# A planned order of all work: one PSUM bank kept for the zero matmuls, less slack behind transfers, and a new order

## The chip, the cores and the metric

The kernel runs on one core of a Trainium2 chip. The metric is device time in microseconds (us) of one execution. A core has five engines with an instruction stream each: TensorE (PE, matrix multiplication into PSUM), VectorE (DVE), ScalarE (ACT), GpSimd (POOL) and SyncE (SP). In this kernel POOL issues all loads, SP issues the stores and the crossbar transposes, and all transfers share 16 DMA engines. PSUM has eight banks of 128 x 512 fp32.

## The reference

Two stages. First a linear attention with an exponential feature map, over 8 batches of 8 heads, 576 tokens, head width 64 and 128 features; then a feed-forward network (FFN) with squared ReLU on 4608 tokens of width 512, inner width 2048.

```python
def phi(x):
    proj = np.einsum('bhsd,df->bhsf', x, w_phi)
    proj = proj - np.max(np.abs(proj), axis=-1, keepdims=True)
    return np.concatenate([np.exp(proj), np.exp(-proj)], axis=-1)
q_p, k_p = (phi(q), phi(k))
kv = np.einsum('bhsf,bhsd->bhfd', k_p, v)
z = np.sum(k_p, axis=2)
num = np.einsum('bhsf,bhfd->bhsd', q_p, kv)
den = np.einsum('bhsf,bhf->bhs', q_p, z)[..., None] + 1e-06
attn = num / den
x = attn.transpose(0, 2, 1, 3).reshape(B * S, H * D)
h = np.maximum(x @ w_in, 0.0)
out = h * h @ w_out
```

All inputs and outputs are fp32; the kernel computes in bf16 and accumulates in fp32.

## The kernel before

The kernel doesn't issue its work in program order. It first describes every operation in a `Plan` (engine, cost, what it reads and writes, which PSUM banks it opens and closes, and a key). `Machine` then plays the plan through once, on the host, at build time: each engine takes the operation with the lowest key among those that are ready, with PSUM banks handed out to PE operations and transfers sharing the DMA engines. What comes out is one order for each engine, and the instructions are written in exactly that order. On the chip each engine goes through its list in order, and waits with semaphores for what an instruction needs. The times of `Machine` fix the order and nothing else, with two exceptions. Loads are held back by a gate, the ACT operation that ends last before the planned start of the load. And zero matmuls are put where PE is planned to idle.

The keys stand in a table `KEYS`, 1739 of them, one for each operation; `RELEASES` has the earliest planned starts of the loads of batches 2 to 7; `STATES` says for each copy or ReLU that either ACT or DVE can do which of the two does it. `SLACK` is added to the planned end of a transfer, by its kind: `first` for the first loads and the weights, `v0` for the first v, `ld` for the loads of batches 2 to 7, `kq` for the crossbar transposes of k and q, `x` for those of the attention's output.

The zero matmuls keep PE busy while it has nothing to do. Before the change the bank they write is any that is planned to be free when PE comes to idle; if none is, there are no zero matmuls in that gap:

```python
spare = next((b for b in range(self.BANKS) if self.free_at[b] <= e["free"] + 1e-9), None) if name == "PE" else None
```

They are written out ahead of each PE operation that is planned before 45 us (`WARM_UP`), as many as fit into the planned gap, at 0.11 us each in the first 6 us and 0.058 us after.

The steps of a batch, with the lines of the kernel before:

- Loads of q, k and v, with a cast to bf16, by POOL (L512, L520, L532); weights (L581, L587).
- Transposes of k and q to kT and qT. In batches 0 and 1 PE does them (L616) with a copy out of PSUM by DVE or ACT (L439, L441); in batches 2 to 7 the crossbar does them (L626).
- Projections of k and q (L670 and L816 in batch 0, L642 elsewhere) that use half of the array's rows, row maxima of their absolute values (DVE L677, L722, L823), exponentials (ACT L705, L728), and v scaled with the exponentials of the maxima (DVE L762, L766).
- KV: 18 matmuls for each pair of heads (L783, L788), 4 pairs to a batch, and a copy to SBUF (L439, L441).
- The features of q, transposed (PE L858, ACT L873), numerators and denominators (PE L888, twice 8 matmuls, with a DVE operation L900 between), the division (DVE L908, L912) and a transpose of the result to xT: on PE (L928, copies L937) in batch 0, by crossbar (L950) elsewhere.
- The FFN in 9 chunks of 512 tokens: first product L1049 in chunk 0 (128 tokens at a time) and L1038 elsewhere, ReLU on ACT (L1015) or DVE (L1017), square on DVE (L1024), second product L1103 (L1067 for the last 128 tokens), copy and store (L1121). Chunk c needs the attention of batch c; the ninth chunk takes the last 64 tokens of all batches.

The FFN of a batch runs among the attention of the following ones. The first FFN matmul, L1049, comes after the attention of batch 0, for which q, k and v must be loaded first.

Of the kernel before, what the change touches and what calls it, by code (L numbers as in the profile page):

```python
# [21 lines left out]
SLACK = {"first": 1.2, "v0": 2.5, "ld": 0.8, "x": 1.2, "kq": 1.0}  # L22
# [3 lines left out]
WARM_UP, COLD = 45.0, 6.0  # L26
# [87 lines left out]
class Machine:  # L114
# [7 lines left out]
    def __init__(self, plan, limits, ahead, patience, want):  # L122
        self.plan, self.limits = plan, limits
        self.ahead, self.patience, self.want = ahead, patience, want
        self.free_at = [0.0] * self.BANKS
        self.holding = None
        self.open = {}
        self.q = {"SP": [], "POOL": []}
        self.q_t, self.q_v = 0.0, 0
        self.hist = {"SP": [], "POOL": []}  # L130
# [64 lines left out]
    def run(self):  # L195
# [81 lines left out]
        while left:  # L277
# [19 lines left out]
            spare = next((b for b in range(self.BANKS) if self.free_at[b] <= e["free"] + 1e-9), None) if name == "PE" else None  # L297
            op = pick(name, e, t)
# [52 lines left out]
def kernel(  # L351
# [245 lines left out]
    def attention(b):  # L597
        s2 = b % 2
        pe_in = b in K['PE_IN']
        first = b == 0  # L600
# [23 lines left out]
        def transposed(x, xt, tag, ttag, key):  # L624
            def fn():
                pin(nc.sync.dma_start_transpose(out=xt, in_=x))  # L626
            add("SP", (2.8 if tag == "xk" else 3.4, 0), key, fn, r=of(tag, b, (0, 1, "s") if tag == "xq" else (0, 1, 2, 3, "s")),
                w=[(ttag, s2, t) for t in range(18)], dma=(3.6, HW_IN, "x", "kq"), what="X" + tag)

        if not pe_in:  # L630
            transposed(xk[s2], kTb, "xk", "kT", KA(b) - 10)
            transposed(xq[s2], qTb, "xq", "qT", KA(b) - 9)
# [345 lines left out]
        else:  # L978
            if pe_in:
# [235 lines left out]
    'PE_IN': [0, 1],  # L1215
    'PX': [1, 1, 1, 1, 1],
# [5 lines left out]
    'LIM': {'b0': 7, 'att': 3, 'kv': 7, 'op': 6},  # L1222
    'AHEAD': 356.131,
    'PATIENCE': 60.701,
# [4 lines left out]
    '1000000100001001111000110100100000000100010000001001000000010101000010000010001000010010000010000000'  # L1229
    '0100000101001010001110100010101001001000100010011001000101001001101010010100101101100010010100011100'  # L1230
    '0111010111100111100110100000111'
# [3 lines left out]
    17407, 102, 303, -19, 23448, 164, 25399, 7284, 103, -334, -342, 962, 612, -4448, -358, -466, 854, -5120, 1043,  # L1235
    1445, 2531, 2378, 1835, 1683, 1283, 2296, 2776, 6225, 1578, 6847, 9430, 23446, 3002, 6973, 2986, 4636, 7251,
    4704, 6911, 3336, 1003, 977, 1014, 1256, 2044, 19225, 3264, 1208, 2649, 9653, 3031, 2018, 7283, 1699, 1392,
    2415, 2482, 2569, 1938, 7416, 2230, 19677, 19665, 21149, 985, 631, 1829, 1167, 502, 1106, 30444, 1429, 24788,
    11688, 1068, 2741, 2271, 1691, 557, 1483, 638, 1830, 1651, 599, -401, 1899, 768, 1607, 1345, 1946, 17315, 1356,
    23984, 24358, 2102, 2748, 1812, 1047, 7206, 3044, 7208, 17205, 16309, 2884, 1937, 2580, 2117, 23465, 1319,  # L1240
    32941, 353, 6936, 22713, 1482, 1252, 12153, 9984, 23851, 1776, 1870, 28693, 2989, 3338, 9168, 2470, 2176, -1818,
    1746, -2214, 2184, 2431, 2073, 16742, 12309, 3675, 32055, 2751, 2607, 33525, 19924, 2061, 1353, 18117, 879, 666,
    2992, 2848, 2951, 3261, 32406, -843, 2706, 724, 5383, 2189, 3713, -1132, 3059, 22482, 2647, 33607, 2425, 2903,
    3153, 7467, 2946, 17043, 887, 30937, 1975, 19418, 5174, 20405, 3839, 537, 22061, 13862, 4153, 4372, 3313, 3702,
    2934, 2946, 2343, 3093, 22612, 3559, 8512, 2725, 3616, 26332, 29011, 3758, 20842, 6383, 2667, 4917, 3013, 11902,
    5345, 5238, 5921, 9912, 17625, 6541, 2315, 4379, 3435, 538, 4929, 3936, -2259, 3063, 3410, 4141, 23913, 13791,
    14506, 9834, 3978, 4002, 4288, 4215, 2945, 1909, 5362, 5104, 5553, 5287, 3268, 17046, 798, 3707, 2741, -1094,
    3553, 8533, 6784, 7264, 5884, 4403, 7199, 11290, 5958, 4782, 5787, 5872, 5644, 5916, 5299, 5137, 5079, 5080,
    20856, -473, 6391, 5749, 5537, 5046, 6063, 19035, 3357, 9582, 5994, 4922, 5968, 6119, 4977, 6670, 6244, 6483,
    6290, 6698, 19067, 4958, -996, 5517, 5252, 5391, 6788, 5266, 4299, 5039, 2805, 10740, 5284, 7476, 6917, 6887,  # L1250
    9690, 7248, 39413, 1751, 9675, 6437, 28262, 6319, 5577, 6334, 6287, 6302, 18429, 7382, 2955, 6913, 5198, 24236,
    28571, 6767, 6251, 7494, -758, 7560, 8050, 9450, 7621, 8371, 7966, 3353, 2499, 2619, 1952, 6194, 29465, 774,
    5220, 3223, 3756, 4311, 3208, 4062, 4051, 4788, 3955, 479, 4014, 3767, 3800, 3168, 4377, -1024, 4889, 5051,
    4450, 2778, 4515, 7272, 9663, 4340, 4251, 5804, 5006, 4304, 9662, 4907, 2794, 5997, 5050, 5175, 5451, 4923,
    28317, 7970, 4699, 4303, 1709, 9057, 5944, 5392, 4331, 14380, 2713, 4765, 4953, 12329, 4480, 5767, 4592, 6860,
    7810, 10905, 2818, 6137, 4180, 2215, 3286, 7321, 5283, 5241, 5956, 5275, 31537, 7305, 7279, 8169, 7954, 8774,
    7928, 7946, 7447, 7197, 8571, 8788, 8754, 9914, 9151, 8623, 10205, 28753, 9236, 8038, 8574, 22052, 8380, 8450,
    7529, 3291, -2, 11359, 9824, 9084, 13735, 9213, 10106, 8801, 8580, 8548, 9717, 12195, 21514, 9841, 10195, 9372,
    20619, 10629, 7364, 7402, 8587, 6358, 6839, 7541, 9500, 9718, 10799, 10955, 10544, 5683, 2374, 9755, 9159,
    27351, 9417, 9862, 9302, 20470, 32494, 10238, 6138, 7030, 7927, 10849, 9641, 9510, -1016, 20794, 10915, 8427,  # L1260
    -116, 13197, 9447, 9495, 2667, 692, 22484, 20389, 10746, 7094, 9290, 10721, 10810, 18159, 12068, 31380, 28083,
    22915, 1026, -887, 11060, 3635, 11045, 11396, 9857, 12004, 7583, 18462, 8756, 4983, 7513, 8752, 3219, 5133,
    6755, -1, 15253, 5347, 6465, 7754, 11386, 4931, 4785, 5572, 8512, 18443, 10833, 15727, 7521, 27495, 8162, 6150,
    7496, 8751, 8038, 7422, 7940, 3836, 10117, 6091, 22706, 7326, 7703, 13090, 9732, 23399, 8450, 13984, 975, 23532,
    8575, 9687, 9024, 7376, 8938, 10675, 9574, 7478, 8651, 8128, 8849, 5308, 31332, 21114, 8850, 29038, 9584, 6298,
    9555, 13221, 10146, 26486, 9580, 10029, 16988, 7506, 5719, 7874, 7841, 7758, 7389, 9044, 16298, 13239, 12245,
    23349, 9079, 12781, 7480, 11973, 8824, 8823, 6561, 6517, 9711, 10208, 3635, 14886, 9819, 5468, 9796, 10776,
    9740, 9730, 27385, 11031, 18006, 10703, 10132, 14, 10657, 9648, 22562, 10246, 19975, 11130, 25441, 23920, 14604,
    8983, 8228, 15704, 10056, 12998, 9196, -1267, 15126, 10713, -326, 20534, 11321, 11509, 12968, 13034, 11538,
    4820, 11603, 1244, 11706, 11438, 11864, 10659, 15019, 12774, 13092, 11103, 11910, 12865, 11965, 11827, 10973,  # L1270
    -497, 11622, 13807, 31538, 11957, 13552, 5263, 12566, 12058, 10811, 25517, 12045, 9673, -2199, 12689, 6817,
    12468, 25073, 13804, 12710, 12761, 14880, 24784, 5370, 9220, 9204, 17211, 13305, -10, 31398, 22456, 9554, 20134,
    14287, 12831, 14375, 12743, 12421, 8816, 16805, 13198, 13168, 9775, 28439, 11026, 24020, 13360, 3050, 15853,
    1925, -239, 4903, 4986, 16708, 13835, 12965, 12562, 11651, 12912, 24547, -1847, 13009, 10966, -2373, 11087,
    9756, 10945, 10200, 12118, 10502, 10956, 21707, 16803, 17099, 11772, 18442, 13381, 11449, 31507, 22778, 12610,
    11775, 11507, 4434, 11804, 11515, 11801, -528, 11413, 13866, 16900, 5711, 15578, 9473, 13709, 19170, 12569,
    10487, 13433, 22777, 22857, 1833, 12762, 24856, 12485, 11283, 14167, 10087, 13341, 8113, 15210, 20080, 16461,
    14025, 15631, 11608, 14097, 7884, 30686, 20661, 25313, -255, -2159, 24682, 11371, 10070, 11200, 16134, 3932,
    16133, 5138, 7416, 7851, 16122, 8358, 8893, 11490, 11992, 12992, 8029, 10687, 6778, 8395, 11617, 11959, 12312,
    760, 4160, 11884, 14072, 15705, 3017, 16120, 11618, 13974, 4928, 13054, 13063, -961, 9709, 13238, 14877, 14414,  # L1280
    14408, 13167, 12813, 14444, 12170, 14604, 5327, 24549, 24508, 27999, 22376, 15936, 15990, 10069, 14146, 14114,
# [97 lines left out]
```

## Time and profile before

| | |
|---|---|
| time, median of 3 | 361.92 us (361.62 to 363.95) |
| span in the profile | 360.4 us |
| PE busy | 346.7 us, 3442 matmuls |
| DVE busy | 292.5 us, 503 instructions |
| ACT busy | 231.9 us, 434 instructions |
| POOL busy | 112.5 us, 167 instructions |
| zero matmuls (L1195) | 118 |
| DMA | 39.62 MB, mean 110 GB/s |

Busy time on PE is not time at PE's peak: a matmul of 512 columns is shown as 379 ns long while the next one starts 216 ns after it. So the distance between starts tells more than the busy share. `PEclk` gives the clock that PE was granted, in tenths of the full one, in 40 slices of 9 us. A row of the table by stretch has first the stretch and its length, then busy us and instructions of PE, PE's weight loads, DVE, ACT and POOL, then PE's clock, the DMA share (16 engines; it counts queues that overlap, so it goes above 1) and GB/s.

### The profile page before, as it was taken

The page shows a single profiled execution, that of the slowest core. Times are in us where ns is not written, and L with a number is a line of the kernel's source. Part 1 is how long each engine was busy: PE and PEld are TensorE (multiplying, and loading weights), DVE is VectorE, ACT ScalarE, POOL GpSimd, SP SyncE. Part 2 cuts the span into 40 slices and gives each one's busy share as a digit, 9 for nine tenths or more (in the row PEclk, how much of TensorE's full clock was granted, in tenths as well). Part 3 has the DMA queues.
Part 4 walks back from the last instruction along what each step waited for, and adds up shares of the span by engine and source line. Part 5 has one row for each costly group of instructions (what it writes and reads, how often), then busy time and mean ns, then how long its engine had stood idle before and what let it go on. Part 6 is the DMA issues. An engine that isn't in the chain of part 4 may idle for free.

```text
span 360.4 us, 8594 instructions
## 1 busy us (share of the span) xinstructions
PE 346.7 (96%) x3442; PEld 198.0 (55%) x3442; DVE 292.5 (81%) x503; ACT 231.9 (64%) x434; POOL 112.5 (31%) x167
## 2 busy tenths in 40 slices
PE   8579999999999999999999999999999999999995
PEld 8368886554554555446544555565455554444444
DVE  4998999899999977899789888999788965686131
ACT  2986899598888783959677847957785340310310
POOL 8626727366636951363415212010000000000000
PEclk9959999999999999999999999999999999999999
DMA  8999999998999999898847774447230031100213
GB/s 96 194 201 136 188 182 117 169 150 107 164 154 126 153 129 188 167 139 121 98 102 96 128 98 104 93 69 122 81 96 2 17 95 45 36 0 2 112 33 89
DMA packets 102632, 39.62 MB, mean 110 GB/s; under 512 B 77249, under 2 KB 98113, under 8 KB 102593
## 3 DMA queue, kind: packets, MB, share of 16 engines
q0 software_dynamic: 51744, 18.36, 47.3%
q1 hardware_dynamic: 50608, 20.55, 25.4%
q8 instruction: 27, 0.44, 0.5%
q10 hardware_dynamic: 240, 0.16, 0.2%
q14 instruction: 13, 0.10, 0.1%
HBM read 36.77 MB, written 9.44 MB: 128 GB/s over the span
## 4 chain that ended last, share of the span: by engine, by line
PE 75%; DVE 11%; ACT 9%; issue 2%; DMA 1%; POOL 0%; DVEq 0%; POOLq 0%; ACTq 0%
PE psum L1103 29%; PE psum L1038 24%; PE psum L888 5%; PE psum L783 4%; DVE mq L823 4%; PE psum L642 3%; PE psum L858 3%; PE psum L1049 2%; ACT kp L728 2%; DVE mk L722 2%; DVE va L766 2%; ACT kn L728 2%; DMA xq<-in_q_dram 1%; DVE h L1024 1%; PE psum L1067 1%
## 5 line engine op out<-in xcount | busy, mean ns | idle before, releaser
L1103 PE MATMUL psum<-wout,h 128*128 128x512 bf16 x560 | 131.5, 379 | 0.0
L1038 PE MATMUL psum<-xT,win 128*128 128x512 bf16 x448 | 105.0, 379 | 0.6 <-ACT hr L1015 0.4
L1015 ACT ACTIVATE hr<-psum 128x512 bf16<-128x512 f32 x91 | 53.6, 598 | 49.7 <-PE psum L1038 26.1
L1103 PEld LDWEIGHTS <-h 128*128 128x128 bf16 x560 | 50.7, 98 | 56.9 <-issue 2.7
L1038 PEld LDWEIGHTS <-win 128*128 128x128 bf16 x512 | 47.5, 98 | 53.6 <-issue 1.6
L1024 DVE TENSOR_TENSOR h<-hr 128x512 bf16<-128x512 bf16 x144 | 56.9, 416 | 16.2 <-ACT hr L1015 15.3
L873 ACT ACTIVATE qp<-psum 128x1024 bf16<-128x1024 f32 (+1 forms) x40 | 37.3, 938 | 20.0 <-PE psum L858 17.4
L532 POOL DMA_DIRECT2D xq<-in_q_dram x52 | 37.6, 726 | 39.1 <-ACT hr L1015 10.3
L823 DVE TENSOR_REDUCE mq<-psum 128x8 f32<-128x1024 f32 (+1 forms) x40 | 43.7, 1110 | 4.6 <-PE psum L642 3.7
L1017 DVE TENSOR_SCALAR hr<-psum 128x512 bf16<-128x512 f32 x53 | 36.1, 683 | 9.8 <-PE psum L1038 8.3
L722 DVE TENSOR_REDUCE mk<-psum 128x8 f32<-128x1024 f32 (+1 forms) x35 | 38.1, 1108 | 2.4 <-PE psum L642 1.7
L728 ACT ACTIVATE kp<-psum 128x1024 bf16<-128x1024 f32 (+1 forms) x35 | 32.8, 937 | 10.2 <-DVE mk L722 10.2
L766 DVE TENSOR_TENSOR va<-xv,va 128x1024 bf16<-128x1024 bf16 (+1 forms) x36 | 38.6, 1101 | 0.6 <-ACT va L747 0.4
L873 ACT ACTIVATE qn<-psum 128x1024 bf16<-128x1024 f32 (+1 forms) x40 | 37.4, 940 | 2.0 <-PE psum L888 2.0
L900 DVE TENSOR_TENSOR psum<-psum,en 128x520 f32<-128x520 f32 (+1 forms) x40 | 27.9, 700 | 7.4 <-PE psum L888 6.4
L728 ACT ACTIVATE kn<-psum 128x1024 bf16<-128x1024 f32 (+1 forms) x35 | 32.9, 948 | 0.1
L912 DVE TENSOR_TENSOR xo<-psum,rden 128x512 bf16<-128x512 f32 (+1 forms) x40 | 27.3, 687 | 0.9
L512 POOL DMA_DIRECT2D xv<-in_v_dram x26 | 18.9, 727 | 28.9 <-ACT qp L873 10.5
L512 POOL DMA_DIRECT2D xk<-in_k_dram x28 | 20.2, 721 | 21.9 <-ACT va L747 7.4
L783 PE MATMUL psum<-va,kp 128*128 128x65 bf16 x256 | 21.1, 199 | 0.1
L783 PE MATMUL psum<-va,kn 128*128 128x65 bf16 x256 | 20.9, 198 | 0.1
L441 ACT ACTIVATE ot<-psum 128x512 f32<-128x512 f32 x24 | 14.4, 603 | 10.0 <-PE psum L1103 6.8
(68 smaller groups left out, 407.4 us busy)
## 6 DMA issues: line engine op xcount, KB each, us to landing
out_dram<-ot SPq DMA_DIRECT2D x32, 256.0 KB, 2.6
xk<-in_k_dram POOLq DMA_DIRECT2D x26, 128.0 KB, 4.4
xv<-in_v_dram POOLq DMA_DIRECT2D x24, 128.0 KB, 4.4
xq<-in_q_dram POOLq DMA_DIRECT2D x48, 64.0 KB, 3.4
win<-in_moe_w_in_dram POOLq DMA_DIRECT2D x4, 512.0 KB, 11.0
wout<-in_moe_w_out_dram POOLq DMA_DIRECT2D x4, 512.0 KB, 7.7
xq<-in_q_dram POOLq DMA_DIRECT2D x4, 256.0 KB, 7.5
xv<-in_v_dram POOLq DMA_DIRECT2D x2, 512.0 KB, 8.5
```

The costliest lines, as they stand in the source:

```text
L512: pin(nc.gpsimd.dma_start(out=x[:, a * 512 : z * 512].rearrange("p (h x) -> p h x", x=4 * D), in_=src[b][2 * a : 2 * z, 0:512, :].rearrang ...
L532: pin(nc.gpsimd.dma_start(out=x[:, jj * 1024 + a * 256 : jj * 1024 + z * 256].rearrange("p (h x) -> p h x", x=128), in_=q[b][2 * a : 2 * z ...
L722: pin(nc.vector.tensor_reduce(out=mk_view(g), in_=ps2(pj)[:, :, : n * Fd].rearrange("p e (i f) -> p e i f", f=Fd), axis=AX.X, op=ALU.max, ...
L728: pin(nc.scalar.activation(out=dst[slot][:, :, :n, :].rearrange("p e i f -> p e (i f)"), in_=ps2(pj)[:, :, : n * Fd], func=ACT.Exp, scale= ...
L766: pin(nc.vector.tensor_tensor(out=o[:, :, :D], in0=xv[s2][:, 512 * g0 : 512 * g1].rearrange("p (m d) -> p m d", d=D), in1=o[:, :, D].to_br ...
L783: pin(nc.tensor.matmul(out=o[:, sg, hi, :], lhsT=(kp, kn)[sg][kgroup[pr]][:, j % 2, 2 * hi + j // 2, :], rhs=va[s2][sg_of(sg, pr)][:, 8 * ...
L823: pin(nc.vector.tensor_reduce(out=mqb[:, c, :, :n], in_=ps2(pj)[:, :, : n * Fd].rearrange("p e (i f) -> p e i f", f=Fd), axis=AX.X, op=ALU ...
L873: pin(nc.scalar.activation(out=o, in_=i_, func=ACT.Exp, scale=sgn))
L1015: pin(nc.scalar.activation(out=hr[sl], in_=ps1(g), func=ACT.Relu))
L1024: pin(nc.vector.tensor_tensor(out=dst, in0=i_, in1=i_, op=ALU.mult))
L1038: pin(nc.tensor.matmul(out=o, lhsT=win[mc // 4][:, kc, mc % 4 * P : (mc % 4 + 1) * P], rhs=x, start=(kc == 0), stop=(kc == KC - 1)))
L1103: pin(nc.tensor.matmul(out=ps1(g), lhsT=h2[c % 2][mc // 4][:, mc % 4, tt * P : (tt + 1) * P], rhs=wout[mc // 4][:, mc % 4, :], start=(mc = ...
```

## The change

Three edits of the planner, and the order that comes of them.

One bank, the eighth, is not handed out before 27 us of the plan (`RESERVED`), and zero matmuls planned before that time write it. So there is always a bank for them in the opening, at the price of one bank fewer for the work. 27 us is about where the FFN begins. The aim is that PE's clock stays up in the opening.

The slack behind transfers is smaller in all five kinds. The aim is that work is planned nearer to the time at which its data is there.

The switch `PE_IN` for batches whose q and k PE transposes is split in one for k (`PE_IN`) and one for q (`PE_Q`). Both name batches 0 and 1, so nothing is computed in another way.

With these a new set of keys, releases and states is given, so every engine's order differs: the order of loads in the opening, the place of each attention step in the FFN, and for some copies and ReLUs the engine (ReLU on DVE 57 times for 53, the output copy 9 times for 11). In the program that results PE has 3543 matmuls for 3442; all 101 more are zero matmuls. The limits on open banks by kind (`LIM`) and two settings of how PE groups its half-array work (`AHEAD`, `PATIENCE`) differ too.

```diff
-SLACK = {"first": 1.2, "v0": 2.5, "ld": 0.8, "x": 1.2, "kq": 1.0}
+SLACK = {"first": 0.6, "v0": 1.0, "ld": 0.6, "x": 1.0, "kq": 0.8}
...
-WARM_UP, COLD = 45.0, 6.0
+WARM_UP, RESERVED, COLD = 45.0, 27.0, 6.0
...
-        self.free_at = [0.0] * self.BANKS
+        self.free_at = [0.0] * (self.BANKS - 1) + [RESERVED]
...
             spare = next((b for b in range(self.BANKS) if self.free_at[b] <= e["free"] + 1e-9), None) if name == "PE" else None
+            if name == "PE" and t < RESERVED:
+                spare = self.BANKS - 1
...
-        pe_in = b in K['PE_IN']
+        pe_in = b in K["PE_IN"]
+        pe_q = b in K["PE_Q"]
...
         if not pe_in:
             transposed(xk[s2], kTb, "xk", "kT", KA(b) - 10)
+        if not pe_q:
             transposed(xq[s2], qTb, "xq", "qT", KA(b) - 9)
...
-            if pe_in:
+            if pe_q:
                 for jj in range(2):
...
     'PE_IN': [0, 1],
+    'PE_Q': [0, 1],
...
-    'LIM': {'b0': 7, 'att': 3, 'kv': 7, 'op': 6},
-    'AHEAD': 356.131,
-    'PATIENCE': 60.701,
+    'LIM': {'tp': 5, 'att': 3, 'kv': 2, 'op': 7},
+    'AHEAD': 290.375,
+    'PATIENCE': 42.743,
...
-    '1000000100001001111000110100100000000100010000001001000000010101000010000010001000010010000010000000'
+    '1000000101101101111011010000100100000010100000000110000000100100000000100010110000000110010000100000'
...
-    17407, 102, 303, -19, 23448, 164, 25399, 7284, 103, -334, -342, 962, 612, -4448, -358, -466, 854, -5120, 1043,
...
-    3918, 5808, 5641, 4331, 5174, 2121, 4913, 2575, 4279, 5137, 5589, 4959, 4761, 3434, 1883, 1066, 401, 1104, 362,
+    1766, 3789, 5898, 5160, 4018, 3823, 3708, 4115, 3210, 5154, 2993, 2851, 3699, 4454, 2664, 1672, 4978, 4723,
...
```

In the plan's own terms the lists `STATES`, `KEYS` and `RELEASES` are replaced whole; only a line of each is shown.

## The prediction

> **What bounds the kernel now.** I read the page first: busy shares, the 40 slices and the chain that ended last.
>
> ```profile
> PE 346.7 (96%) x3442; PEld 198.0 (55%) x3442; DVE 292.5 (81%) x503; ACT 231.9 (64%) x434; POOL 112.5 (31%) x167
> ...
> PEclk9959999999999999999999999999999999999999
> ...
> PE 75%; DVE 11%; ACT 9%; issue 2%; DMA 1%; POOL 0%; DVEq 0%; POOLq 0%; ACTq 0%
> ```
>
> TensorE (PE) is the bound, but the third slice shows it at half clock. Next, busy time by stretch (busy us of each engine, instructions, then clock, DMA share, GB/s):
>
> ```profile
> 0.00:9.00 9.00, 7.79 (x94) 7.41 (x95) 4.10 (x11) 2.58 (x4) 7.92 (x16) 1.00 0.89 96
> 9.00:18.00 9.00, 5.18 (x77) 3.48 (x75) 8.41 (x15) 8.72 (x21) 5.81 (x9) 0.91 1.49 194
> 18.00:27.00 9.00, 6.44 (x92) 6.04 (x92) 8.71 (x15) 7.75 (x23) 2.55 (x4) 0.53 1.35 201
> 27.00:36.00 9.00, 9.00 (x175) 7.86 (x172) 7.77 (x20) 5.99 (x14) 6.23 (x9) 1.00 1.18 136
> ...
> 108.00:144.00 36.00, 36.00 (x381) 19.48 (x378) 31.36 (x53) 26.07 (x48) 19.76 (x29) 1.00 1.15 149
> ```
>
> Two regimes. From 9 to 27 us PE idles while VectorE (DVE) and ScalarE (ACT) are full; from 27 us on PE is full. To ask whether "full" hides slack I take start-to-start times from long runs in the chain of waits:
>
> ```profile
> 46.05 4.47 PE psum L1049 x80
> ...
> 316.69 8.63 PE psum L1038 x40
> ...
> 342.59 10.36 PE psum L1103 x48
> ...
> 352.95 3.51 PE psum L1067 x32
> ```
>
> That is 0.0559, 0.2158, 0.2158 and 0.110 us per matmul. The first FFN matmul (L1049) starts at 33.20 us, the last one ends at 352.95 + 3.51 = 356.46: a stretch of 323.3 us. Its own work, by the counts in the instruction order: 560 x 0.2158 + 512 x 0.2158 + 256 x 0.0559 + 32 x 0.110 = 249.2 us of FFN, and about 62 us of attention (600 matmuls of L888 at 0.031, 28 KV groups at 0.71, 504 of L642 at 0.028, 70 of L858 at 0.11, 32 transposes at 0.056). 311.3 in all; the other 12 us are 98 changes between half-array and whole-array matmuls (about 0.1 each, 10 us) and holes of about 2 us. The stretches agree: from 27 to 351 us PE is idle 2.2 us. So **after the first FFN matmul there is almost nothing to win; what can move the time down is when that matmul starts.** The 3.9 us from the last matmul to the end of the span are a copy and a store.
>
> The opening, us by us:
>
> ```profile
> 14.00:15.00 1.00, 0.00 (x0) 0.09 (x1) 1.00 (x4) 1.00 (x4) 1.00 (x3) 1.00 1.30 196
> ...
> 20.00:21.00 1.00, 0.00 (x0) 0.00 (x0) 1.00 (x3) 1.00 (x4) 0.00 (x0) 0.50 1.26 210
> ...
> 25.00:26.00 1.00, 1.00 (x21) 1.00 (x19) 1.00 (x2) 0.35 (x2) 0.34 (x1) 0.50 1.55 193
> ...
> 28.00:29.00 1.00, 1.00 (x27) 1.00 (x27) 0.55 (x1) 0.49 (x1) 0.81 (x2) 1.00 1.23 130
> ```
>
> PE is idle at 14 us and again at 20, the clock is 0.50 from about 16.4 to 26.5 us, and DVE and ACT are full until 24. Only from 21.6 to 27.4 us does PE lead and the others wait for it.
>
> **What the Trainium skill says.** "TensorE: Matmul & The Clock Gate", Part 1, says the array falls to half clock after an idle window of about 3.4 us and comes back after a busy one. The trace agrees in kind: sparse work from 13.9 us, half clock 2.4 us later; dense from 21.6, full clock 5 us later. KV matmuls (L783) step 0.055 us at half clock and 0.030 after. The same page ("Engine queue depths") says ACT and DVE take their instructions strictly in order, and that matmuls stay in program order: a wait holds up all behind it. "DMA: Bandwidth & Descriptors" (Issuing engines are not separate DMA queues) has all issuers share 16 DMA engines. The trace fits: a kT crossbar transpose lands 4.5 to 8.5 us after issue.
>
> **The change, part by part.**
>
> *Zero matmuls.* The order holds 118 zero matmuls before, 219 after, all ahead of the first FFN matmul. They go where before had no bank to put them: 49 in a row ahead of a q projection, 12 and 18 around the last k transposes, where the trace of before shows 14 to 21 us idle. 101 more x 0.056 = 5.7 us of PE time, beside the DVE and ACT work that fills 11 to 24 us; so they cost nothing as long as that work is what PE waits for. What they buy: L816, L858 and three KV groups from 21.6 to 27.4 ran at half clock. KV: three groups at 1.1 instead of 0.68 = 1.3 us; L816 with L858, 1.86 instead of about 0.93 = 0.9 us. Up to 2.2 us, of which DVE, idle for 0.2 us at 24.9 and 0.9 us at 27.6 to 28.5, can follow by only about 1.1.
>
> *Bank 7 withheld until 27 us.* It leaves three pairs for the wide projections. No new instruction; the order already includes it. Nothing, since DVE and ACT, not banks, fill the opening.
>
> *Order of the loads.* Before, a 32 KB v load is issued at 1.25 us and the first k load at 2.00; after, the first k load and the first q load are each one issue (0.75 us) earlier, so q lands at 8.08 - 0.75 = 7.3. The identity (affine select, 5.74 + 0.35 = 6.09 us, what the first transpose at 6.30 waited for) comes after three loads instead of six. Only 34 zero matmuls stand ahead of the first transpose instead of 52, 18 x 0.105 = 1.9 us less. The last 128 KB of k are queued behind v and a weight load now: 2.1 MB into the queue, where before the second q load stood, which landed near 17.7. PE's turn for them comes at about 18, so a wait of 0 to 0.7 us; I take 0, as 12 and 18 zero matmuls stand around it.
>
> *First FFN matmul, after, from PE's own list.* 34 zero matmuls from 0.99 us at 0.105 end at 4.6; four transposes, 10 zero matmuls, 8 projections end near 6.2; then PE waits for q until 7.3. Behind it stand 175 zero matmuls (175 x 0.058 = 10.2), real work of 11.7 and 20 array changes (2.4) = 24.3: 31.6. Some 15 blocks of zero matmuls leave up to one matmul of gap each, say 0.06: **32.5, against 33.2**. From the other side, DVE: 22.8 us of its instructions stand ahead of the first xT copy against 22.3 before (two more copies of kv, one more L900, one narrow reduce later). It was full but for 2.3 us between 8.6 and 32.2, starts 0.75 earlier, and loses about 1.1 of its idle: -0.75 + 0.5 - 1.1 = -1.3. The two bounds give -0.7 and -1.3; PE's is the later, so I take -0.7.
>
> *Less time kept free behind transfers.* After the first FFN matmul the work is the same (311.4 against 311.3; 96 array changes against 98). Only waits can differ. For the 12 crossbar loads of kT and qT of batches 2 to 7 I add up the PE work between what the last load is held for and the first matmul that reads the tile: 18.1 us on average before (least 12.6), 15.4 after (least 12.7). The chain it must cover: issue 0.7, load 4.4, transpose 5.2 to 8.5 = 10.3 to 13.6. The two shortest of before, 12.6 each, met no PE wait on a DMA. PE behind such a wait is the whole FFN, so it costs its full length. Bounds: 0, and two or three transposes landing as late as the worst (2 us each), 5 us. From xo to its FFN matmul the least is 4.9 before, 5.1 after; from KV to L888 it falls from 0.3 to 0, about 0.3 us once. I take 0 net.
>
> *Copies that change engine.* ReLU 53 to 57 on DVE, output copies 11 to 9, and four others: +0.9 us of DVE in 292. Nothing, since DVE is idle 4 to 5 us in each 36 of the FFN.
>
> Sum: 361.9 - 0.7 = **361.2**.
>
> **Rivals.** *Both ends tighten* (0.20): the earlier opening (-0.7) and half of the 2.2 us of holes gone (-1.1): 360.1. For it: fewer array changes and a full clock. Against: nothing in the order aims at those holes. *Slack becomes waits* (0.18): -0.7 and two late crossbar transposes at 1.5 us: 363.4. For it: leads 2.7 us shorter, traffic of 150 GB/s while they run. Against: no such wait before at leads of 12.6. *Zero matmuls in the way* (0.12): PE's list runs late by the wait for q and the fillers do not shrink, so the first FFN matmul starts near 34.2 instead of 33.2: 362.9. For it: the first two q loads were already waited for. Against: DVE and ACT are full there. My forecast has 0.50.
>
> **Numbers.** The holes bound the gain: the opening by PE's list at about -1.0 and holes -2.2 give 358.7, so over 1% faster (under 358.3) has 0.04. Over 1% slower (above 365.5) needs three late transposes, 0.08. Range: down to 359.0, up to two transposes 2 us late, 364.4.
>
> **What would show it.** Right: no 5 in PEclk after the first 5 us; L1049 starting at 32 to 33; KV groups at 0.6 to 0.7 us from the first; PE waits on DMA under 1 us; 27 to 351 us idle for 2 us. Wrong: L1049 later than 33.5, or PE waits on kT or qT in the FFN stage of over 2 us in sum; or the stretch after L1049 shorter than 321 us.

## The result, and the profile after

| | before | after |
|---|---|---|
| time, median | 361.78 us (361.54 to 363.95, 6 runs) | 367.93 us (366.55 to 369.38, 6 runs) |
| span in the profile | 360.4 us | 366.0 us |
| first FFN matmul starts | 33.20 us | 32.57 us |
| last matmul ends | 356.44 us | 362.04 us |
| the stretch between | 323.24 us | 329.47 us |

The ratio is **1.0157, 95% interval 1.0124 to 1.0191: slower**, clear of the noise though under 2%. The forecast was 361.2 us. In these two profiles the opening came out as forecast, 0.63 us earlier; the stretch behind it, forecast unchanged, is 6.2 us longer. The last copy and store take 3.9 us in both. Ratios leave out runs over 1.5% above the fastest of the same kernel, which concerns one kernel below, that with gates 1 us earlier (371.02 and 372.04 us, two of six runs; with them its ratio would be 1.013 to 1.015).

The page of the kernel after (its lines are numbered 4 above those of before, as L1042 for L1038):

```profile
PE 349.4 (95%) x3508; PEld 201.1 (55%) x3543; DVE 293.4 (80%) x504; ACT 232.0 (63%) x433; POOL 112.4 (31%) x167
...
PEclk9999999999999999999999999999999999999999
...
PE 52%; DVE 12%; ACT 11%; DMA 11%; issue 8%; POOL 3%; SPq 0%; DVEq 0%; POOLq 0%; ACTq 0%
```

The 5s in the clock are gone. But for the zero matmuls of PE and 0.9 us on VectorE no engine has more work, yet in the chain that ended last PE falls from 75% to 52% and DMA rises from 1% to 11%. (Of 3543 matmuls 35 have no record; small holes ended by "issue" are such gaps. The loads of weights into the array are all there.)

The table by stretch, first the opening and two stretches of the FFN:

```profile
9.00:18.00 9.00, 8.95 (x147) 7.60 (x146) 8.57 (x15) 8.24 (x20) 4.87 (x9) 1.00 1.45 196
18.00:27.00 9.00, 8.38 (x151) 6.44 (x149) 8.58 (x14) 7.79 (x21) 5.78 (x9) 1.00 1.39 196
...
72.00:81.00 9.00, 6.83 (x75) 3.62 (x71) 6.88 (x8) 8.35 (x17) 3.40 (x6) 1.00 1.28 182
108.00:144.00 36.00, 33.21 (x335) 17.67 (x335) 29.56 (x50) 26.24 (x46) 21.68 (x32) 1.00 1.19 148
```

Then the whole from 27 to 351 us, before and after:

```profile
27.00:351.00 324.00, 321.81 (x3149) 177.22 (x3146) 269.49 (x462) 212.44 (x389) 96.25 (x140) 1.00 0.70 106
```

```profile
27.00:351.00 324.00, 313.94 (x3075) 174.12 (x3107) 270.11 (x463) 211.06 (x385) 93.83 (x137) 1.00 0.74 105
```

PE is busy 8.95 and 8.38 of 9 us in the opening, where it had 5.18 and 6.44 (the zero matmuls count as busy). But from 27 to 351 us it idles 10.1 us in place of 2.2 (at least 1.1 of them are gaps of missing records), and the stretch from 108 to 144 us, which had no hole before, has 2.8 us of them. At the same rate of DMA traffic, 148 GB/s for 149: it isn't more traffic.

What PE waited for, in the view of waits (engine, line, what ended the wait: us in all, times, longest):

```profile
PE psum L1042 <- DMA xT<-xo: 2.5, 2, 2.1
PE psum L862 <- DMA qT<-xq: 1.5, 1, 1.5
PE psum L619 <- DMA xq<-in_q_dram: 1.2, 2, 0.7
...
PE psum L1042 <- ACT ot L443: 0.5, 1, 0.5
PE psum L1042 <- DVE ot L441: 0.4, 1, 0.4
```

Single transposes and loads missed their time. (Of the 1.2 us for q, 0.7 lie in the opening, where they were forecast.) The wait of 2.1 us is at 79.92 us: an xT transpose issued at 73.74 landed at 79.87, after 6.1 us. The other knot, a place where several waits meet, is at 117 to 124 us, where the two waits for ot, the output tile, belong too. The timeline of SyncE, GpSimd and VectorE there (start, duration, instruction, and in brackets the idle time ahead and what ended it):

```profile
105.53 6.33 SPq L629 DMA_TRANSPOSE qT<-xq  x1
```

```profile
108.01 0.70 POOL L514 DMA_DIRECT2D xv<-in_v_dram  x1 [1.82 <-ACT kp L732]
108.92 0.71 POOL L534 DMA_DIRECT2D xq<-in_q_dram  x1 [0.21 <-issue]
109.84 0.69 POOL L514 DMA_DIRECT2D xk<-in_k_dram  x1 [0.21 <-issue]
117.64 0.69 POOL L534 DMA_DIRECT2D xq<-in_q_dram  x1 [7.10 <-DMA qT<-xq]
```

```profile
116.12 2.37 DVE L770 TENSOR_TENSOR va<-xv,va 128x1024 bf16<-128x1024 bf16 x2 [2.33 <-DMA xv<-in_v_dram]
118.40 0.69 DVE L441 COPY ot<-psum 128x512 f32<-128x512 f32 x1
```

Eight loads were issued from 102.7 to 109.8 us, around one qT transpose. The transpose took 11.5 us to land (105.53 to 117.08), the v load issued at 108.01 took 8.0; VectorE came to its tile at 113.79, 5.8 us after the issue. Behind the v load VectorE stands for 2.3 us, then comes the copy of ot out of PSUM, and PE's next L1042 waits for that bank. Behind the transpose stand PE (1.5 us) and, for 7.1 us, GpSimd's next q load, whose tile the transpose still reads.

The landing times over the whole run, before and then after, from the list of DMA issues (count, then the median us from issue to landing):

```profile
xT<-xo SPq DMA_TRANSPOSE x28, 2.6
...
qT<-xq SPq DMA_TRANSPOSE x6, 5.2
```

```profile
xT<-xo SPq DMA_TRANSPOSE x28, 3.6
...
qT<-xq SPq DMA_TRANSPOSE x6, 7.2
```

Not every kind of transfer took longer: the medians of kT and xS fell, from 6.5 to 5.9 us and from 3.7 to 2.8, and that of the 128 KB loads of v from 4.4 to 4.0.

To see where in the work the 6.2 us were lost, I added up the counted work (the durations of the prediction) ahead of each of PE's weight loads and took the time since the first FFN matmul less that sum. Against before, in us, good to about 0.4, with two of the experiments below:

| counted work, us | 40 | 50 | 70 | 80 | 100 | 170 | 220 | 310 |
|---|---|---|---|---|---|---|---|---|
| after | +0.3 | +2.6 | +1.6 | +3.6 | +4.8 | +5.1 | +5.4 | +6.2 |
| after, no v loads, no crossbar reads | -0.3 | -0.1 | -0.8 | -0.9 | -0.2 | +0.2 | +0.5 | +0.9 |
| after, gates 4 us earlier | -0.3 | -0.1 | -0.9 | -1.0 | -0.4 | -0.2 | -0.4 | +0.8 |

The loss comes in two steps, at the two knots, and a slope behind them. The slope, some 1.4 us from 100 on, is in the other two rows as well (1.1 and 1.2), so it isn't one of late transfers. Nor do both steps stand in every execution: in a second profile of after (365.48 us, stretch 327.1) the xT transpose of the first knot landed in 4.1 us, and PE didn't wait for it; the second knot was there again, with VectorE idle for 2.2 us for the same v load.

### The profile page after: what moved, and what is told of

It reads as the page before. It is cut to its first block, busy times and chain, and to the rows that moved or that the text cites. A ratio compares the mean times of both kernels' runs of the same rounds, so it can differ in the third digit from the quotient of the medians.

```text
span 366.0 us, 8767 instructions
## 1 busy us (share of the span) xinstructions
PE 349.4 (95%) x3508; PEld 201.1 (55%) x3543; DVE 293.4 (80%) x504; ACT 232.0 (63%) x433; POOL 112.4 (31%) x167
## 4 chain that ended last, share of the span: by engine, by line
PE 52%; DVE 12%; ACT 11%; DMA 11%; issue 8%; POOL 3%; SPq 0%; DVEq 0%; POOLq 0%; ACTq 0%
PE psum L1107 22%; PE psum L1042 19%; DMA xv<-in_v_dram 4%; PE psum L892 4%; DMA xT<-xo 3%; DVE h L1028 3%; DVE mq L827 2%; ACT hr L1019 2%; PE psum L646 2%; DVE va L770 2%; DVE hr L1021 2%; PE psum L862 2%; DMA xk<-in_k_dram 2%; DVE mk L726 1%; DMA xq<-in_q_dram 1%
## 5 line engine op out<-in xcount | busy, mean ns | idle before, releaser
L1107 PE MATMUL psum<-wout,h 128*128 128x512 bf16 x525 | 128.4, 379 | 2.7 <-issue 1.1
L1042 PE MATMUL psum<-xT,win 128*128 128x512 bf16 x448 | 105.5, 379 | 3.7 <-DMA xT<-xo 2.5
L1019 ACT ACTIVATE hr<-psum 128x512 bf16<-128x512 f32 x87 | 50.9, 601 | 48.7 <-PE psum L1042 29.8
L1042 PEld LDWEIGHTS <-win 128*128 128x128 bf16 x512 | 47.9, 98 | 58.5 <-issue 6.2
L1028 DVE TENSOR_TENSOR h<-hr 128x512 bf16<-128x512 bf16 x144 | 57.0, 417 | 12.7 <-ACT hr L1019 11.9
L1021 DVE TENSOR_SCALAR hr<-psum 128x512 bf16<-128x512 f32 x57 | 38.6, 685 | 9.6 <-PE psum L1042 8.4
L443 ACT ACTIVATE ot<-psum 128x512 f32<-128x512 f32 x26 | 15.5, 602 | 24.8 <-PE psum L1107 19.2
L787 PE MATMUL psum<-va,kp 128*128 128x65 bf16 x256 | 19.9, 194 | 0.2 <-ACT hr L1019 0.2
L787 PE MATMUL psum<-va,kn 128*128 128x65 bf16 x256 | 19.9, 193 | 0.0
```

The source lines that it names most:

```text
L787: pin(nc.tensor.matmul(out=o[:, sg, hi, :], lhsT=(kp, kn)[sg][kgroup[pr]][:, j % 2, 2 * hi + j // 2, :], rhs=va[s2][sg_of(sg, pr)][:, 8 * ...
L1019: pin(nc.scalar.activation(out=hr[sl], in_=ps1(g), func=ACT.Relu))
L1021: pin(nc.vector.tensor_scalar(out=hr[sl], in0=ps1(g), scalar1=0.0, scalar2=None, op0=ALU.max))
L1028: pin(nc.vector.tensor_tensor(out=dst, in0=i_, in1=i_, op=ALU.mult))
L1042: pin(nc.tensor.matmul(out=o, lhsT=win[mc // 4][:, kc, mc % 4 * P : (mc % 4 + 1) * P], rhs=x, start=(kc == 0), stop=(kc == KC - 1)))
L1107: pin(nc.tensor.matmul(out=ps1(g), lhsT=h2[c % 2][mc // 4][:, mc % 4, tt * P : (tt + 1) * P], rhs=wout[mc // 4][:, mc % 4, :], start=(mc = ...
```

## The experiments

**What PE waits for.** First the crossbar alone: matmuls of L646, L862 and L1042 read a weight tile in place of what the crossbar wrote.

```diff
-pin(nc.tensor.matmul(out=o[:, e, i * Fd : (i + 1) * Fd], lhsT=xt[r, t, :],
+lhs = xt[r, t, :] if b < 2 else win[t % 4][r, t // 4 % 4, :P]
+pin(nc.tensor.matmul(out=o[:, e, i * Fd : (i + 1) * Fd], lhsT=lhs,
...
+if b >= 2:
+    rhs = win[c % 4][r, c // 4, : n * P].rearrange("p (i x) -> p i x", x=P)
...
-x = xS[:, :, kc, :] if c == NCH - 1 else xT[c % NXT][kc // 2][:, :, kc % 2, :]
+x = win[kc][:, c % 4, :].rearrange("p (t x) -> p t x", x=P)
```

> The changed kernel with its order kept on every engine. The projections of batches 2 to 7 and the FFN of chunks 1 to 8 read a weight tile in place of kT, qT, xT and xS, so no matmul waits for a crossbar transpose; the transposes still run. (It leaves out the use of those tiles: the output is another.) Theory 'late transposes': the stretch from the first to the last FFN matmul, 329.5 us in the changed kernel, falls by 5 to 6 us to about 324, and the time from 367.9 to about 362. Rival 'other waits of the new order' (banks, copies, DVE and ACT): it stays within 1.5 us of 367.9.

Measured: 366.87 us, 1.0121 (1.0072 to 1.0170), stretch 327.3 us. The same edit in the kernel before:

> Control: the kernel before with the same edit (matmuls of batches 2 to 7 and chunks 1 to 8 read a weight tile in place of the crossbar's tiles; the output is another). Theory 'late transposes': the kernel before waited little for them, so it gains at most 1 us: 361 to 362. If it gains 3 us or more, both kernels pay for the crossbar and the difference lies elsewhere.

Measured: 362.18 us, 0.9994 (0.9983 to 1.0006), stretch 323.3 us. So before pays nothing for its crossbar, and after seems to pay some 1.3 us that the edit gives back (the intervals with and without it meet, so this size isn't sure); most of the loss stayed. The wait of 1.5 us for qT was gone, and another, for ot, was in its place, at 117.8 us (the one for q lies in the opening):

```profile
PE psum L619 <- DMA xq<-in_q_dram: 2.4, 1, 2.4
PE psum L1045 <- DVE ot L441: 2.2, 1, 2.2
```

That is the v load, by way of VectorE, which stood 2.6 us for it. My theory at that time, late transposes alone, fell: at the same place a load was late too. So next the v loads, alone and with the crossbar reads:

```diff
             def fn(a=a, z=z):
+                if tag == "xv" and b >= 2:
+                    return
                 pin(nc.gpsimd.dma_start(
```

> Edit: the kernel after, with the v loads of batches 2 to 7 (about 96 KB to a pair of heads and half a batch) left out; V is scaled from what lies in the tile, so the output differs. Every engine's order stays. Theory A (what after loses in its FFN stretch is time in which TensorE waits, at the end of a chain, for transfers of any kind that are in flight together): a v load can no longer be late, and the crossbar transposes beside them land sooner, so at least half of the 6.2 us comes back: 363.5 to 365, stretch 324.5 to 326.5. Rival B (the loss lies in the order of compute work: copies out of PSUM and bank changes that come later on VectorE and ScalarE): at most 0.8 us comes back, 367 or more.

> Edit: the kernel after with no v loads in batches 2 to 7, and with TensorE reading a weight tile in place of what the crossbar wrote (kT and qT of batches 2 to 7, xT and xS); both left out of the result. Orders stay. Theory A: no transfer after the opening is waited for but q and k of batch 1, so the stretch goes to 323.5 to 325 and the time to 361.5 to 363. Rival B: the crossbar alone gave back about 1 us and stretch 327.3, and this gives no more than 0.8 on top: 365 to 366.5.

(The size in the first of these is wrong: the list of issues has 24 v loads of 128 KB and 16 of 32 KB.) Measured: 364.47 us, 1.0054 (1.0038 to 1.0069), stretch 326.4 us; and 363.65 us, 1.0020 (1.0011 to 1.0029), stretch 324.2 us. From 27 to 351 us PE of the second idles 2.4 us:

```profile
27.00:351.00 324.00, 321.61 (x3139) 176.98 (x3137) 270.76 (x465) 211.18 (x385) 70.27 (x102) 1.00 0.61 94
```

Theory A holds in its main part (363.65 us is a little above its 361.5 to 363): of the 6.2 us, some 5 go with these transfers. By the ratios it is 1.37 of 1.57 percentage points, 5.0 us; by the profiles 5.3, but the profiled run was the fastest of 22. About 1 us remains that they don't make; I put it down to the order of the compute work, but didn't take it apart. Do v loads cost by being waited for, or by slowing others? Here they were to run as in after, into a tile that nobody reads:

```diff
-x = dst[b % 2]
+x = (xw if tag == "xv" and b >= 2 else dst)[b % 2]
```

> Edit: the kernel after, with the v loads of batches 2 to 7 written to a tile that nothing reads; V is scaled from what lies in the old tile, so the result leaves v of these batches out. The loads are issued as in after and move the same bytes; no order changes. Without the loads the time fell from 1.0157 to 1.0054 times that of before, about 3.7 us. Theory C (what v loads cost is traffic: they run beside crossbar transposes, which land later, and TensorE waits for those): the loads still run, so little comes back: 366.5 to 368 (1.012 to 1.016), and the xT, kT and qT transposes land as late as in after. Rival D (what they cost is the wait of VectorE for v at 116 us, and what is held up behind it): most comes back without them being gone: 364 to 365.3 (1.005 to 1.008).

Measured: 366.62 us, 1.0115 (1.0092 to 1.0138), stretch 326.2 us in the profiled run, the fastest of six. By its number D, the wait alone, falls, and C, the traffic, is just met. But the loads did not run as in after. The v load of the second knot was issued only when the qT transpose beside it had nearly landed (112.35 us, landing 112.81), and held back the q and k loads behind it on GpSimd:

```profile
112.35 0.70 POOL L515 DMA_DIRECT2D xw<-in_v_dram  x1 [8.13 <-ACT va L752]
```

In after it goes out 2.48 us behind the issue of that transpose, here 8.95 us behind. So this run doesn't part the wait from the traffic, and the question stays open.

**The three parts of the change apart.** The bank and its zero matmuls, in the kernel before (the keys are the planned starts of before, so that its order nearly stays):

```diff
-WARM_UP, COLD = 45.0, 6.0
+WARM_UP, RESERVED, COLD = 45.0, 27.0, 6.0
...
+            if name == "PE" and t < RESERVED:
+                spare = self.BANKS - 1
```

> Edit: the kernel before with the reserved bank and its zero matmuls (253 of them for 118), its own slack and, but for about 33 operations, its own order. My theory: the opening gains what it gained in after (first FFN matmul at 32.3 to 32.9 for 33.2, clock full from the start), the stretch stays 323 to 324: 360.8 to 361.6. Rival: zero matmuls in the way or one bank fewer: first FFN matmul at 33.8 or later, 362.5 or more.

Measured: 362.53 us, 1.0004 (0.9985 to 1.0023); first FFN matmul at 32.87 us, stretch 323.4 us, clock full. 135 more zero matmuls cost nothing that shows. The 0.3 us by which the first FFN matmul comes earlier are less than the times can show, and less than that start varies: with the opening of before unchanged it was at 32.53 us in before without crossbar reads, and at 33.87 in before with earlier gates, below. The slack in before, and the old slack in after:

```diff
-SLACK = {"first": 1.2, "v0": 2.5, "ld": 0.8, "x": 1.2, "kq": 1.0}
+SLACK = {"first": 0.6, "v0": 1.0, "ld": 0.6, "x": 1.0, "kq": 0.8}
```

> Edit: the kernel before with after's five smaller values of SLACK; its own order but for about 46 of 1739 operations. Theory A1 (the slack values make transfers late whatever the order): stretch 325 or longer, 363.5 or more. Theory A2 (it is after's order, where loads stand and how short before their use, and not the five numbers): stretch 323 to 324, 361.3 to 362.3.

> The order of the changed kernel, given as keys (each operation's key is its planned start), planned again with the old slack (1.2, 2.5, 0.8, 1.2, 1.0). Few operations move: 8 of 88 on SP, 12 of 435 on ACT, 21 of 504 on DVE, 5 of 163 on POOL, 9 of 549 groups on PE. Theory 'the slack taken away is the loss': those moves are the ones that matter, and the time falls by 3 us or more, to under 365. Theory 'the order is the loss, and 0.2 us of slack for a transpose is too little either way': within 1.5 us of 367.9.

Measured: before with the new slack 364.17 us, 1.0045 (1.0028 to 1.0062), first FFN matmul at 33.67 us, stretch 324.6 us, with

```profile
PE psum L1038 <- DMA xT<-xo: 1.5, 2, 0.9
```

where before had no such row. After with the old slack: 366.75 us, 1.0121 (1.0077 to 1.0166). So in before the five numbers cost about 0.4 points, between A1 and A2. In after the old ones take off about as much, but over four runs, with an interval that meets that of after, so this half isn't shown. The larger rest of the 1.57 points I put down to after's order, by difference. A wider slack for the crossbar isn't a cure:

```diff
-SLACK = {"first": 0.6, "v0": 1.0, "ld": 0.6, "x": 1.0, "kq": 0.8}
+SLACK = {"first": 0.6, "v0": 1.0, "ld": 0.6, "x": 3.0, "kq": 4.5}
```

> The order of the changed kernel as keys, planned with much more slack behind crossbar transposes: 3.0 us for xT (1.0) and 4.5 us for kT and qT (0.8), about what the late ones took beyond the usual. 57 of 549 groups on PE move behind others. Theory 'late transposes': PE finds other work in front of most late tiles; 4 of the 6 us come back: about 364. Rival 'other waits of the new order': no gain, 367 to 369.

Measured: 374.28 us, 1.0331 (1.0307 to 1.0355), a clear miss. In the profile PE's waits for transfers come to 1 us, for q and k; the long ones are for ACT and VectorE:

```profile
PE psum L1042 <- ACT hr L1019: 2.1, 3, 1.5
PE psum L1042 <- ACT qn L877: 1.4, 2, 0.7
PE psum L892 <- DVE psum L904: 1.3, 2, 0.9
```

Slack makes the planner put the users of a transfer later, and so moves the whole order; it doesn't make the transfer start earlier.

**When the loads start.** The gate of a load is an ACT operation. Moving it to an earlier one changes no order on any engine and no byte, only the time of issue:

```diff
 for a in reversed(acts):
-    if a.at + a.lat <= t + 1e-9:
+    if a.at + a.lat <= t - 4.0:
         op.gate = a
         break
```

> Edit: the kernel after; each held-back load of batches 2 to 7 waits for the ACT operation that ends last before the planned start less 4 us, in place of the planned start itself. Order, bytes and everything else as in after. Theory E (the loads are issued too near to their use): v at 116 us is no longer waited for, and the transposes that follow a load start earlier: 363.5 to 365.5. Rival F (the loads were early enough, a mean of 15 to 40 us ahead of their use; what is late are the crossbar transposes, whose place is set by the queue of SyncE, and moving loads only moves the traffic): 366 to 369, waits in other places.

Measured: **363.56 us, 1.0033 (1.0018 to 1.0048)**, stretch 324.1 us. About 4.5 us came back. (Its profiled run, too, is the fastest of 22.) Its row from 27 to 351 us, then from its timeline the v load of the second knot and its reader on VectorE, then its landing times:

```profile
27.00:351.00 324.00, 321.62 (x3134) 176.71 (x3132) 270.64 (x464) 211.00 (x385) 94.03 (x137) 1.00 0.71 105
```

```profile
101.45 0.70 POOL L514 DMA_DIRECT2D xv<-in_v_dram  x1 [0.66 <-ACT en L834]
```

```profile
111.09 2.35 DVE L770 TENSOR_TENSOR va<-xv,va 128x1024 bf16<-128x1024 bf16 x2
```

```profile
xT<-xo SPq DMA_TRANSPOSE x28, 3.2
...
qT<-xq SPq DMA_TRANSPOSE x6, 7.3
```

The same v load is issued 9.6 us ahead of the operation that reads it; in after it was 5.8 (108.01 to 113.79, when VectorE came to it). It landed after 6.7 us. The qT transpose of this batch still took 10.5 us, and the median is as high as in after: the transfers aren't much quicker, they are just early enough. The xT transpose that had cost 2.1 us lands in 4.0 us (71.67 to 75.62), but it did so in the second profile of after as well, so that isn't the gates' doing. Then doses, and after once more, to see whether the chip made the difference:

> Edit: the kernel after with the gates of the loads of batches 2 to 7 set to 2 us ahead of the planned start (4 us gave 1.0033, 0 gives 1.0157). Theory E (time ahead of use, dose by dose): about half way, 1.006 to 1.011, 364 to 366. Rival G (chance: which transposes happen to fall among which loads): anywhere, with no order by dose; 1.012 or more, or 1.003 or less, speaks for it.

> Edit: as above with 8 us. Theory E: no worse than with 4 us, 1.001 to 1.004, 362 to 363.5, and less scatter between runs; GpSimd may wait for buffers to come free, which holds up its other work. Rival G: 1.006 or more.

> No edit: the kernel after once more, beside the next run on one chip, since the runs with earlier gates were on other chips than the first. Theory E: 1.012 to 1.019 again. If the chip or the day made the loss: 1.008 or less.

> Edit: the kernel after with its gates 1 us earlier (0 gave 1.0157; 2, 4 and 8 us gave 1.0034, 1.0033 and 1.0020). Theory E with a threshold (a few transfers miss their use by 1 to 2 us, the rest had room): between, 1.006 to 1.012. Rival G (any shift breaks up the one bad meeting of loads and transposes): 1.004 or less already.

The last column follows the v load of the second knot in each profile: time from its issue until VectorE comes to its tile, time it took to land, and how long VectorE stood.

| gates earlier by | time, us | ratio | 95% interval | v load: lead, landing, wait (us) |
|---|---|---|---|---|
| 0, first | 367.93 | 1.0157 | 1.0124 to 1.0191 | 5.8, 8.0, 2.3 |
| 0, again | 367.62 | 1.0156 | 1.0113 to 1.0198 | 5.8, 7.8, 2.2 |
| 1 us | 366.16 (4 runs) | 1.0099 | 1.0066 to 1.0132 | 6.7, 9.2, 2.6 |
| 2 us | 364.84 | 1.0034 | 1.0018 to 1.0051 | 7.6, 8.2, 0.7 |
| 4 us | 363.56 | 1.0033 | 1.0018 to 1.0048 | 9.6, 6.7, 0 |
| 8 us | 363.97 | 1.0020 | 1.0002 to 1.0037 | 10.4, 8.3, 0 |

The loss repeats, and is mostly gone from 2 us on. The steps from 0 to 1 us and from 2 to 8 us lie within the intervals; the fall from 1 to 2 us is clear of them. For 1 us and 8 us chance (rival G) had named other numbers; at 2 us neither G's nor mine was met, for the loss isn't in proportion to the time. I read it as a threshold, and the last column agrees: the load takes 7 to 9 us to land at every dose, and a lead of 5.8 or 6.7 us is too short for that, 7.6 nearly long enough. (Medians come from different chips; the ratios are against before on the same chip.) The control:

> Edit: the kernel before with its gates 4 us earlier. Theory E: before already has its margin (its TensorE waits for no transfer over 0.4 us in the FFN stretch), so the same time within 0.2%: 361.3 to 362.3. Rival G: other meetings of loads and transposes, so a change either way of 0.3% or more.

Measured: 363.85 us, 1.0016 (1.0005 to 1.0027). Before had its margin, and earlier gates are no gain in themselves; in this profile they even come with a wait of PE of 1.0 us for an xT, at 118 us, that before doesn't have.

**Both halves together.** The opening of after, and before's order and later slacks behind it; the keys are the planned starts. In words:

```diff
-key = before's planned start
+key = after's planned start if that is below 28 us, else before's - 0.8 us
```

> Edit: a kernel that takes the keys, engines and first two slacks of after for what after plans before 28 us, with the reserved bank, and the order of before, shifted by 0.8 us, for all that follows, with before's slack for batches 2 to 7. If the gain of after's opening (0.6 us) and the stretch of before (323.2 us) can be had together: first FFN matmul at 32.4 to 32.9, 360.8 to 361.5 where before is at 361.8 (0.997 to 0.999). If a few operations at the seam come out of step: 362 to 364.

> Edit: the hybrid (opening of after, order of before behind it, 1.0008) with its gates 4 us earlier. Its profile showed the first FFN matmul at 32.4 and one wait of 0.8 us for an xT transpose at 78 us. Theory E: that wait goes, 0.996 to 0.999 of before, 360.6 to 361.6, faster than both. Rival G: 1.000 to 1.004.

Measured: 363.11 us, 1.0008 (0.9994 to 1.0022), with PE waiting 0.8 us for an xT at 78 us; and with earlier gates 362.83 us, **0.9987 (0.9975 to 0.9999)**, where that wait is gone (stretch 323.5 us). This is the one kernel ahead of both, by 0.1%, and its interval only just leaves 1 out.

## Why the prediction was wrong

- **Bound and lever: half right.** PE is the bound, and no work was added. But "what can move the time down is when that matmul starts" looked only down; there was far more room upward, in a stretch with 2 us of holes.
- **Zero matmuls, bank, load order, first FFN matmul at 32.5: right in kind, and lucky in the tenths.** 32.57 us was measured, q was waited for until 7.39 (7.3 forecast), clock full, KV groups at 0.6 to 0.7 us. But over ten profiles with after's opening this start lies between 32.33 and 34.32 us (median 32.65), and over three with before's at 32.53, 33.20 and 33.87. In the two latest of the ten PE stood 2.1 and 2.4 us for the first q. So one pair of profiles can't show a gain of 0.6 us, nor part it between the bank and the load order.
- **"Less time kept free behind transfers ... I take 0 net": the step that failed.** The term was +6.2 us: some 5 that go with the v loads and the crossbar's tiles and about 1 that stays when they are gone. The bound of 5 us counted two or three crossbar transposes of k and q, as if only these could be late. In the profiles an xT transpose, a q load, and VectorE standing in order behind one v load had their part. I had the mean lead fall by 2.7 us, and set that against a least lead that didn't fall (12.6 and 12.7) and landing times of 5.2 to 8.5 us taken from before. In after one qT took 11.5 us, with seven loads under way beside it at some time, and the v load of the same knot 8.0 us against a lead of 5.8. I had asked for no lead of a load to its reader on VectorE at all. A lead is no margin unless the landing time is known for the place where the transfer will run.
- **"From xo to its FFN matmul the least is 4.9 before, 5.1 after": right and not enough.** One landed in 6.1 us, and cost 2.1 us in that execution.
- **"the work is the same" after the first FFN matmul: the counts hold, but about 1 us is lost** that neither counted work nor array changes nor these transfers show. Its cause stays open.
- **Copies that change engine: +0.9 us of VectorE, as said** (293.4 us); that it costs nothing wasn't tested.
- **Rivals.** "Slack becomes waits" named the right mechanism, with the wrong size (363.4) and too few victims. "Zero matmuls in the way" fell: the first FFN matmul came earlier. "Both ends tighten" fell.
- **Signs.** "PE waits on DMA under 1 us" and "27 to 351 us idle for 2 us" failed, and told it: 5.4 us (0.7 of them the forecast wait for q) and 10.1. The signs named for "wrong" did not fire: kT and qT cost 1.5 us, not over 2. They watched two tiles, and xT, q and v were late too.

## What to carry to other kernels

In a kernel with an order fixed beforehand, ask of every transfer not only how long before its use it starts, but how long such transfers take at that place, and what stands behind its reader on an in-order engine. A hole-free trace says that the margins were enough, not how wide they are; moving the gates alone, by 1, 2, 4 and 8 us, measures them cheaply. Slack in a planner that moves the readers isn't lead for the transfer. And before a knot in one trace is called the loss, look whether a second execution has it.

## What I had not expected of the hardware

- By issues and landings in the trace of after: qT transposes that had three or more loads under way beside them at some time took 9.2 us in the mean (4 of them, longest 11.5), with fewer 5.8 (2); xT and xS transposes 4.1 (17) and 3.0 (18). In before: 5.2 (2) and 5.1 (4) for qT, 3.9 (15) and 2.5 (20) for xT and xS. Company is thus not the whole of it: one qT of before was issued with five loads in flight and landed in 5.2 us, and a transfer that takes longer meets more others. What made the slow ones slow isn't shown.
- The same order of instructions gives another time, by where transfers land: after ran from 365.48 to 370.37 us in twelve runs, and without v loads and crossbar reads from 362.65 to 364.49 in 22. But with gates 4 us earlier it still ran from 362.20 to 367.14 in 22, so scatter alone doesn't tell thin margins.
